# A weight's low part on GpSimd instead of VectorE, in attention with two networks behind it

## The chip, the cores and the metric

The kernel runs on one core of a Trainium2 chip. The metric is the time of one execution on the device, in microseconds (us). Its engines are TensorE (PE in the rows, PEld for its weight loads), VectorE (DVE), ScalarE (ACT), GpSimd (POOL) and SyncE (SP, which issues transfers). Each engine works through its own queue in order; a semaphore holds an instruction until what it needs is there, and everything behind it on the same engine waits too.

## What is computed

Attention over 2 batches, 8 heads, 768 positions and 64 columns with a window of 128 positions and 4 sink positions, then a network with a squared ReLU, then one with a rational function. Inputs are float32 or float64; the weights come as float64.

```python
def _attn_ref(q, k, v, n_sink, window):
    scores = scale * np.matmul(q, k.transpose(0, 1, 3, 2))
    keep = is_sink | in_window
    scores = np.where(keep, scores, -1000000000.0)
    scores = scores - np.max(scores, axis=-1, keepdims=True)
    a = np.exp(scores)
    a = a / (np.sum(a, axis=-1, keepdims=True) + 1e-09)
    return np.matmul(a, v).astype(np.float32)
...
def _moe_ref(x, w_in, w_out):            # x: 1536 x 512, w_in: 512 x 2048, w_out: 2048 x 512
    h = x @ w_in
    r = np.maximum(h, 0.0)
    g = r * r
    return (g @ w_out).astype(np.float32)
...
def _moe2_ref(x, w_in, w_out, a, b):
    h = x @ w_in
    h2 = h * h
    h3 = h2 * h
    P = a[0] + a[1] * h + a[2] * h2 + a[3] * h3
    Q = 1.0 + np.abs(b[0]) * np.abs(h) + np.abs(b[1]) * h2
    g = P / (Q + 1e-06)
    return (g @ w_out).astype(np.float32)
```

## The kernel before

**Stages.** The 1536 rows of tokens are four groups of 512, 256, 256 and 512. Attention is cut into 24 units of two heads by two blocks of 128 queries. The eight units of group 0 run at the start, up to about 56 us. From then on the first network works on group 0, later on groups 1, 2 and 3, and the units of the later groups are put between its steps, piece by piece. Behind it, from about 370 us, stands the second network.

**A unit of attention.** Scores (line 298) on TensorE; mask and row minimum on VectorE (line 307); exponential with row sums on ScalarE (line 309, four to a unit); reciprocal of the sums on VectorE (lines 312, 313); scaling by them (line 317), two pieces on GpSimd and two on VectorE; transposes on TensorE (line 330), whose results are copied out as `pT0` by ScalarE and as `pT1` by VectorE (line 332); product with the values (line 345), copied out as `xhi` and `xlo` (lines 350, 351) or `x` (line 353).

**Products in two parts.** A float32 product is three products of a fast type: each operand is split in a high part, rounded, and a low part, the remainder. A step of the first network takes 128 of the 2048 middle columns: `gemm1` multiplies `whi` by `xhi`, `whi` by `xlo` and `wlo` by `xhi` (lines 411 to 413), `act1` makes the square of the ReLU as `ghi` and `glo` (lines 420 to 423), and `gemm2a` multiplies these by the second matrix two steps later (lines 434, 435 and 440).

**A weight's conversion.** A weight tile of 128x512 comes as float64 by one transfer of 512 KB into `st` (three buffers). `to_f32` makes a float32 of it: ScalarE casts the top half-word into `top` (line 135, a single buffer), VectorE shifts and combines `st` and `top` into `wt` (line 136, two buffers). Then `w_split_` has ScalarE round it to `whi` (line 395) and VectorE take `wlo` = `wt` - `whi` (line 396). There are 64 such conversions, 32 for each network. Of the first network's, seven run during the units at the start (`CONV`), and 25 in the steps of group 0, from about 58 to 127 us; all stay in SBUF. The second network's 32 run later, from within the last group on.

**What sets the order.** A scheduler lays out the queues of VectorE, ScalarE, GpSimd and SyncE. TensorE's queue is written by hand up to group 2. `issue_after(op)` lets the scheduler place an instruction only behind the named one. The conversions of the first network are held behind the mask (`lastV`) and the exponentials (`lastA`) of a recent piece of attention in this way: `va_hist` keeps these two for each piece, and `w_split` takes those of three pieces ago.

Of the kernel before, what the change touches and what calls it, by code (L numbers as in the profile page):

```python
# [10 lines left out]
F32 = mybir.dt.float32  # L11
# [6 lines left out]
ALU = mybir.AluOpType  # L18
# [20 lines left out]
NORM_POOL = (0,)  # L39
# [24 lines left out]
def seg_dims(seg):  # L64

    _, blk0, nb = seg
    assert nb == 2
    return (2 * KB + P, nb * P, 3 * P, 4 * P) if blk0 > 0 else (KB + P, nb * P, 2 * P, 2 * P)


def key_cols(seg, i, j):

    _, blk0, _ = seg
    if blk0 == 0 and i == 0:
        return 0, P
    return (i if blk0 > 0 else 0) * KB + j * D, WQ
# [52 lines left out]
def to_f32(nc, st, t, top):  # L129

    mid = st.bitcast(I32)[:, 1 : 1 + 2 * WH].rearrange("p (n w) -> p n w", w=2)[:, :, 0]
    head = st.bitcast(BF16)[:, 4 : 4 + 4 * WH].rearrange("p (n w) -> p n w", w=4)[:, :, 0]
    nc.scalar.copy(top.bitcast(F16).rearrange("p (n w) -> p n w", w=2)[:, :, 1], head)  # L135
    nc.vector.scalar_tensor_tensor(t.bitcast(I32), in0=mid, scalar=13, in1=top,  # L136
                                   op0=ALU.logical_shift_right, op1=ALU.bitwise_or)
# [20 lines left out]
class Fast:  # L158
# [116 lines left out]
    def att_unit(self, u, raws, alt):  # L275


        nc = self.nc
        tags = self.alt_tags(alt)
        V, A, G = nc.vector, nc.scalar, nc.gpsimd  # L280
        g, c, seg, xo = u
        b, blk0, nb = seg
        wk, wq, wa, wb = seg_dims(seg)
        n = nb * P
        raw, vv = raws
        kr, qr = raw[:, :wk], raw[:, wk:]
        rows = [slice(D * k, D * k + D) for k in range(2)]
        ws = [key_cols(seg, i, 0)[1] for i in range(nb)]
        os = [sum(ws[:i]) for i in range(nb)]
        pt = self.att.tile([P, 2, 2 * WQ], F32, tag="p", name="p", bufs=2)  # L290
        sums = self.const.tile([P, 4], F32, tag="sums", name="sums", bufs=6)
        sc = [self.att_bank() for _ in range(2)]
        for i in range(nb):
            for k, r in enumerate(rows):
                for j in range(2):
                    q0 = i * P + j * D
                    off, w = key_cols(seg, i, j)
                    nc.tensor.matmul(sc[k][j * D : j * D + D, os[i] : os[i] + w], qr[r, q0 : q0 + D],  # L298
                                     kr[r, off : off + w], start=True, stop=True, skip_group_check=True)
        for i in range(nb):  # L300
            m = self.m2 if blk0 > 0 else (self.m0, self.m1)[i]
            for k in range(2):
                mn = self.mn[:, self.mn_i : self.mn_i + 1]
                self.mn_i += 1
                cs = slice(os[i], os[i] + ws[i])
                p = pt[:, k, cs]
                self.lastV = V.tensor_tensor_reduce(p, sc[k][:, cs], m, scale=-0.125, scalar=3.0e38,  # L307
                                                    op0=ALU.add, op1=ALU.min, accum_out=mn)
                self.lastA = A.activation(p, p, AF.Exp, scale=-1.0, bias=mn,  # L309
                                          accum_out=sums[:, k * nb + i : k * nb + i + 1])  # L310
        yield
        V.tensor_scalar_add(sums[:, : 2 * nb], sums[:, : 2 * nb], 1e-9)
        V.reciprocal(sums[:, : 2 * nb], sums[:, : 2 * nb])  # L313
        for i in range(nb):
            for k in range(2):
                p = pt[:, k, os[i] : os[i] + ws[i]]
                (G if i in NORM_POOL else V).tensor_scalar(p, p, sums[:, k * nb + i : k * nb + i + 1], 0.0,  # L317
                                                           op0=ALU.mult, op1=ALU.add)
        if g:
            for _ in range(ST_T):  # L320
                yield
            vv = self.att_load_v(u, 0)
        yield
        heads = [i for i in range(nb) if ws[i] == WQ]
        pieces = [os[i] + x for i in range(nb) for x in ((0, P - NSK) if i in heads else (0,))]
        pT = []
        for k in range(2):
            tb = self.att_bank()
            for j, o in enumerate(pieces):
                nc.tensor.transpose(tb[:, j * P : (j + 1) * P], pt[:, k, o : o + P], self.ident)  # L330
            t = self.att_tile(f"pT{k}", len(pieces) * P, alt=tags[k])
            (A.copy if k == 0 else V.tensor_copy)(t, tb[:, : len(pieces) * P])
            pT.append(t)
        yield
        va, vb = (t.rearrange("p (j d) -> p j d", d=D) for t in vv)
        ob = self.att_bank()
        if blk0 > 0:
            jobs = [(va, 0, 0, 0, D), (vb, 0, P, 0, D), (vb, 1, D, D, D), (va, 1, P + D, D, P)]
        else:
            jobs = [(va, 0, 0, 0, P + D)]  # L340
        y, pp = 2 * len(heads) - 2, (len(pieces) - 2) * P
        jobs += [(vb, y, pp + P, P, D), (vb, y + 1, pp + D, P + D, D), (va, len(heads), pp + P + D, P + D, D)]
        for n_, (vt, vi, pp, q0, w) in enumerate(jobs):
            for k, r in enumerate(rows):
                nc.tensor.matmul(ob[r, q0 : q0 + w], vt[:, 2 * vi + k], pT[k][:, pp : pp + w], start=n_ == 0,  # L345
                                 stop=n_ == len(jobs) - 1, skip_group_check=True)
        xs = slice(xo, xo + n)
        if g == 0:
            xhi, xlo = self.x[g]
            A.copy(xhi[:, c, xs], ob[:, :n])  # L350
            V.tensor_tensor(xlo[:, c, xs], ob[:, :n], xhi[:, c, xs].bitcast(F32), op=ALU.subtract)
        else:
            A.copy(self.x32[g][:, c, xs], ob[:, :n])
        yield
# [32 lines left out]
    def w_split_(self, which, f, half):  # L387
        nc = self.nc
        st = self.wst.pop((which, f, half))
        t = self.stage.tile([P, WH], F32, tag="wt", name="wt", bufs=2)  # L390
        to_f32(nc, st, t, self.tops[self.conv_i % NTOP])
        self.conv_i += 1
        whi = self.wp.tile([P, WH], F32R, tag=f"whi{f}_{half}", name="whi")
        wlo = self.wp.tile([P, WH], F32R, tag=f"wlo{f}_{half}", name="wlo")
        nc.scalar.copy(whi, t)  # L395
        nc.vector.tensor_tensor(wlo, t, whi.bitcast(F32), op=ALU.subtract)  # L396
        self.w[(which, f, half)] = (whi, wlo)


# [76 lines left out]
    def run(self, ctx):  # L476
        tc, nc = self.tc, self.nc
        V, A = nc.vector, nc.scalar
# [8 lines left out]
        self.psum = mk(root, "psum", 1, None, space=bass.MemoryType.PSUM)  # L487
        self.att_banks, self.h_banks = [0, 1, 2, 3, 6, 7], [4, 5]
        self.att_i = self.h_i = 0
        self.lastV = self.lastA = None  # L490
        self.va_hist = []
        self.a2i = 0
        self.x, self.x32, self.w, self.wst = {}, {}, {}, {}
# [35 lines left out]
        def tick():  # L529
            with ExitStack() as c:  # L530
                if urgent:
                    c.enter_context(tc.high_priority(offset=HP))
                tick_()
            self.va_hist.append((self.lastV, self.lastA))

        def tick_():
            nonlocal done, tick_no, ui
# [61 lines left out]
        with tc.manual_schedule(engines={mybir.EngineType.PE}):  # L599
            for k in range(n0 + 1):  # L600
                if k == 0:
                    wload(0, 3)
                if k < n0:
                    u, raws = loaded.pop(0)
                    g0[k] = self.att_unit(u, raws, k % NALT)
                    for _ in range(2):
                        next(g0[k])
                if k:
                    with tc.high_priority(offset=HP0):
                        next(g0[k - 1])  # L610
                while k >= 2 and pc < (k - 1) // per:
                    for f in range(HEAD):
                        self.gemm1_part(0, f, pc, self.x[0], GN[0], hb[f])
                    pc += 1
                if k:
                    with tc.high_priority(offset=HP0):
                        next(g0[k - 1])
                with ExitStack() as cc:
                    cc.enter_context(tc.issue_after(self.lastV.ins))
                    cc.enter_context(tc.issue_after(self.lastA.ins))  # L620
                    for _ in range(CONV[k]):
                        wconv(*cq[0][0])
                while nload < n0 and len(loaded) < DEPTH - 1 or not loaded:
                    prefetch()
            done = n0
# [133 lines left out]
        for i in range(len(steps) + 1):  # L759
            if i < len(steps):  # L760
                which, t, f = steps[i]
# [253 lines left out]
```

## Time and profile before

| | us |
|---|---|
| time, median of three runs | 639.09 (638.14 to 640.57) |
| time of the profiled execution | 640.31 |
| its span in the profile | 638.5 |
| TensorE busy in it | 614.0 |
| VectorE busy | 417.3 |
| ScalarE busy | 416.9 |
| GpSimd busy | 109.1 |

The profile is of one execution. Its span runs from the first to the last instruction; the time of that execution is 1.8 us longer. TensorE is busy for 96% of the span, VectorE and ScalarE for 65% each, GpSimd for 17%. These shares are means over stages that differ, so the rows below take the stages apart. In the rows, "idle before" is the time an engine stood still ahead of an instruction, and behind the arrow stands the instruction that released it.

### The profile page before, as it was taken

The page shows a single profiled execution, that of the slowest core. Times are in us where ns is not written, and L with a number is a line of the kernel's source. Part 1 is how long each engine was busy: PE and PEld are TensorE (multiplying, and loading weights), DVE is VectorE, ACT ScalarE, POOL GpSimd, SP SyncE. Part 2 cuts the span into 40 slices and gives each one's busy share as a digit, 9 for nine tenths or more (in the row PEclk, how much of TensorE's full clock was granted, in tenths as well). Part 3 has the DMA queues.
Part 4 walks back from the last instruction along what each step waited for, and adds up shares of the span by engine and source line. Part 5 has one row for each costly group of instructions (what it writes and reads, how often), then busy time and mean ns, then how long its engine had stood idle before and what let it go on. Part 6 is the DMA issues. An engine that isn't in the chain of part 4 may idle for free.

```text
span 638.5 us, 10295 instructions
## 1 busy us (share of the span) xinstructions
PE 614.0 (96%) x3841; PEld 513.2 (80%) x3841; DVE 417.3 (65%) x854; ACT 416.9 (65%) x896; POOL 109.1 (17%) x123
## 2 busy tenths in 40 slices
PE   4698999999999999999999999999999999999996
PEld 3466777877999899998888888888888888888885
DVE  6766887733242353346666559998788777877773
ACT  4567888845454555456777768777676666766663
POOL 2110000000010011021000003434223332222221
PEclk9888999999999999999999999999999999999998
DMA  8734677621221232003555500000010000100001
GB/s 291 272 114 148 220 235 249 225 88 35 57 76 52 82 106 80 1 1 133 184 191 193 191 1 1 1 0 1 0 67 2 0 1 0 55 12 2 1 1 69
DMA packets 19351, 54.86 MB, mean 86 GB/s; under 512 B 2528, under 2 KB 3808, under 8 KB 19296
## 3 DMA queue, kind: packets, MB, share of 16 engines
q1 hardware_dynamic: 19008, 54.01, 25.4%
q8 instruction: 32, 0.52, 0.4%
q14 instruction: 23, 0.19, 0.1%
q10 hardware_dynamic: 288, 0.13, 0.1%
HBM read 50.99 MB, written 3.15 MB: 85 GB/s over the span
## 4 chain that ended last, share of the span: by engine, by line
PE 92%; ACT 3%; DVE 3%; DMA 1%; issue 0%; POOL 0%; POOLq 0%
PE b L411 14%; PE b L413 13%; PE b L412 13%; PE b L434 7%; PE b L440 7%; PE b L435 7%; PE b L473 7%; PE b L472 7%; PE b L471 7%; PE b L345 4%; PE b L298 3%; PE b L330 2%; ACT p L309 2%; DVE p L307 1%; DMA nsw<-nsw 1%
## 5 line engine op out<-in xcount | busy, mean ns | idle before, releaser
L411 PE MATMUL b<-xhi,whi 128*128 128x512 f32 (+1 forms) x320 | 113.7, 356 | 0.5 <-ACT xhi L350 0.5
L412 PE MATMUL b<-xlo,whi 128*128 128x512 f32 (+1 forms) x320 | 111.8, 349 | 0.0
L413 PE MATMUL b<-xhi,wlo 128*128 128x512 f32 (+1 forms) x320 | 111.7, 349 | 0.0
L423 DVE TENSOR_TENSOR glo<-b,ghi 128x512 fp32r<-128x512 f32 (+1 forms) x64 | 35.5, 555 | 76.4 <-ACT b L422 76.2
L434 PE MATMUL b<-ghi,whi 128*128 128x512 f32 (+1 forms) x256 | 83.7, 343 | 0.8 <-ACT ghi L421 0.8
L435 PE MATMUL b<-ghi,wlo 128*128 128x512 f32 (+1 forms) x256 | 81.9, 336 | 0.0
L462 POOL TENSOR_TENSOR glo<-t,ghi 128x512 fp32r<-128x512 f32 x34 | 45.0, 1323 | 213.6 <-ACT ghi L461 187.2
L472 PE MATMUL b<-wlo,ghi 128*128 128x512 f32 x192 | 74.7, 389 | 0.0
L471 PE MATMUL b<-whi,ghi 128*128 128x512 f32 x192 | 74.4, 389 | 0.0
L473 PE MATMUL b<-whi,glo 128*128 128x512 f32 x192 | 71.9, 389 | 0.0
L411 PEld LDWEIGHTS b<-xhi,whi 128*128 128x128 f32 x320 | 60.8, 190 | 10.7 <-issue 2.2
L413 PEld LDWEIGHTS b<-xhi,wlo 128*128 128x128 f32 x320 | 60.9, 190 | 7.7
L412 PEld LDWEIGHTS b<-xlo,whi 128*128 128x128 f32 x320 | 60.9, 190 | 7.3
L317 POOL TENSOR_SCALAR p<-p,sums 128x224 f32<-128x224 f32 (+1 forms) x48 | 25.4, 541 | 232.8 <-DVE sums L313 127.4
L309 ACT ACTIVATE p<-p,mn 128x224 f32<-128x224 f32 (+1 forms) x96 | 43.9, 459 | 32.1 <-DVE mn L307 32.0
L396 DVE TENSOR_TENSOR wlo<-wt,whi 128x512 fp32r<-128x512 f32 x64 | 44.7, 699 | 25.5 <-ACT whi L395 25.2
L395 ACT CAST whi<-wt 128x512 fp32r<-128x512 f32 x64 | 39.5, 618 | 33.3 <-PE b L412 21.1
L420 ACT ACTIVATE b<-b 128x512 f32<-128x512 f32 (+1 forms) x64 | 31.0, 486 | 43.6 <-PE b L413 43.6
L440 PE MATMUL b<-glo,whi 128*128 128x512 f32 (+1 forms) x256 | 55.9, 340 | 0.0
L434 PEld LDWEIGHTS b<-ghi,whi 128*128 128x128 f32 x256 | 48.4, 189 | 8.4 <-issue 2.0
L435 PEld LDWEIGHTS b<-ghi,wlo 128*128 128x128 f32 x256 | 48.5, 189 | 4.9
L135 ACT CAST top<-st 128x512 f16<-128x512 bf16 x64 | 49.7, 776 | 1.0 <-DVE wt L136 1.0
(128 smaller groups left out, 1242.0 us busy)
## 6 DMA issues: line engine op xcount, KB each, us to landing
st<-w SPq DMA_DIRECT2D x64, 512.0 KB, 3.5
vv<-att SPq DMA_DIRECT2D x12, 448.0 KB, 3.3
raw<-att SPq DMA_DIRECT2D x12, 352.0 KB, 3.2
out<-o SPq DMA_DIRECT2D x8, 256.0 KB, 2.1
raw<-att SPq DMA_DIRECT2D x6, 272.0 KB, 3.8
vv<-att SPq DMA_DIRECT2D x6, 256.0 KB, 3.7
raw_e<-att SPq DMA_DIRECT2D x4, 352.0 KB, 5.5
vb<-att SPq DMA_DIRECT2D x4, 256.0 KB, 4.5
```

What stands on the lines that cost most here:

```text
L135: nc.scalar.copy(top.bitcast(F16).rearrange("p (n w) -> p n w", w=2)[:, :, 1], head)
L309: self.lastA = A.activation(p, p, AF.Exp, scale=-1.0, bias=mn, accum_out=sums[:, k * nb + i : k * nb + i + 1])
L411: nc.tensor.matmul(h[:, :n], whi[:, cs], xhi[:, c, :n], start=(c == 0), stop=False)
L412: nc.tensor.matmul(h[:, :n], whi[:, cs], xlo[:, c, :n], start=False, stop=False)
L413: nc.tensor.matmul(h[:, :n], wlo[:, cs], xhi[:, c, :n], start=False, stop=(c == NC - 1))
L434: nc.tensor.matmul(acc[m], whi[:, ms], ghi, start=(f == 0 and not pk), stop=pk, **kw)
L435: nc.tensor.matmul(acc[m], wlo[:, ms], ghi, start=False, stop=pk, **kw)
L440: nc.tensor.matmul(acc[m], whi[:, ms], glo, start=False, stop=pk or f == NF - 1, **kw)
L462: self.lastL = nc.gpsimd.tensor_tensor(glo, t3, ghi.bitcast(F32), op=ALU.subtract)
L471: nc.tensor.matmul(acc[t], ghi[:, ts_], whi, start=(f == 0), stop=False)
L472: nc.tensor.matmul(acc[t], ghi[:, ts_], wlo, start=False, stop=False)
L473: self.lastM = nc.tensor.matmul(acc[t], glo[:, ts_], whi, start=False, stop=(f == NF - 1))
```

## The change

The subtraction of line 396 goes to GpSimd where the weight is one of the first network's (`which` is 0); the second network's stay on VectorE. The last scaling that a unit of attention puts on GpSimd (line 317) is remembered as `lastP`, and a conversion is held behind it as it is behind `lastV` and `lastA`. Line numbers from 319 on are two higher in the changed kernel, those from 490 on up to three (the subtraction is line 398 there).

```diff
--- before.py
+++ after.py
@@ -314,8 +314,10 @@
         for i in range(nb):
             for k in range(2):
                 p = pt[:, k, os[i] : os[i] + ws[i]]
-                (G if i in NORM_POOL else V).tensor_scalar(p, p, sums[:, k * nb + i : k * nb + i + 1], 0.0,
-                                                           op0=ALU.mult, op1=ALU.add)
+                op = (G if i in NORM_POOL else V).tensor_scalar(p, p, sums[:, k * nb + i : k * nb + i + 1], 0.0,
+                                                                op0=ALU.mult, op1=ALU.add)
+                if i in NORM_POOL:
+                    self.lastP = op
         if g:
             for _ in range(ST_T):
                 yield
@@ -393,7 +395,7 @@
         whi = self.wp.tile([P, WH], F32R, tag=f"whi{f}_{half}", name="whi")
         wlo = self.wp.tile([P, WH], F32R, tag=f"wlo{f}_{half}", name="wlo")
         nc.scalar.copy(whi, t)
-        nc.vector.tensor_tensor(wlo, t, whi.bitcast(F32), op=ALU.subtract)
+        (nc.vector if which else nc.gpsimd).tensor_tensor(wlo, t, whi.bitcast(F32), op=ALU.subtract)
         self.w[(which, f, half)] = (whi, wlo)
 
 
@@ -487,7 +489,7 @@
         self.psum = mk(root, "psum", 1, None, space=bass.MemoryType.PSUM)
         self.att_banks, self.h_banks = [0, 1, 2, 3, 6, 7], [4, 5]
         self.att_i = self.h_i = 0
-        self.lastV = self.lastA = None
+        self.lastV = self.lastA = self.lastP = None
         self.va_hist = []
         self.a2i = 0
         self.x, self.x32, self.w, self.wst = {}, {}, {}, {}
@@ -531,7 +533,7 @@
                 if urgent:
                     c.enter_context(tc.high_priority(offset=HP))
                 tick_()
-            self.va_hist.append((self.lastV, self.lastA))
+            self.va_hist.append((self.lastV, self.lastA, self.lastP))
 
         def tick_():
             nonlocal done, tick_no, ui
@@ -618,6 +620,7 @@
                 with ExitStack() as cc:
                     cc.enter_context(tc.issue_after(self.lastV.ins))
                     cc.enter_context(tc.issue_after(self.lastA.ins))
+                    cc.enter_context(tc.issue_after(self.lastP.ins))
                     for _ in range(CONV[k]):
                         wconv(*cq[0][0])
                 while nload < n0 and len(loaded) < DEPTH - 1 or not loaded:
```

The scheduler gives all queues but the pinned one of TensorE anew. TensorE's order stays. In the rows of the order below, numbers behind a name tell buffers of the same name apart.

**GpSimd, from the units at the start to the end of group 0's steps.** `p` are a unit's exponentials, `sums` their reciprocals, `wlo` the low parts. The queue of the kernel before:

```order
L317 TENSOR_SCALAR p_577<-p_577,sums_578 128x224 x2
L317 TENSOR_SCALAR p_834<-p_834,sums_835 128x224 x2
L317 TENSOR_SCALAR p_988<-p_988,sums_989 128x224 x2
L317 TENSOR_SCALAR p_1167<-p_1167,sums_1168 128x224 x2
L317 TENSOR_SCALAR p_1353<-p_1353,sums_1354 128x224 x2
```

The same stretch of the changed one:

```order
L398 TENSOR_TENSOR wlo_828<-wt_824,whi_827 128x512
L317 TENSOR_SCALAR p_834<-p_834,sums_835 128x224 x2
L398 TENSOR_TENSOR wlo_879<-wt_875,whi_878 128x512
L398 TENSOR_TENSOR wlo_906<-wt_902,whi_905 128x512
L398 TENSOR_TENSOR wlo_934<-wt_930,whi_933 128x512
L398 TENSOR_TENSOR wlo_955<-wt_951,whi_954 128x512
L398 TENSOR_TENSOR wlo_983<-wt_979,whi_982 128x512
L398 TENSOR_TENSOR wlo_1028<-wt_1024,whi_1027 128x512
L317 TENSOR_SCALAR p_988<-p_988,sums_989 128x224 x2
L398 TENSOR_TENSOR wlo_1056<-wt_1052,whi_1055 128x512
L398 TENSOR_TENSOR wlo_1097<-wt_1093,whi_1096 128x512
```

Between two pairs of scalings there are now five to seven subtractions.

**ScalarE, where the first network takes over from the units at the start.** `b4`, `b5`, `b6` are the results of `gemm1`, `ghi_701` is the high part of the first step's squared ReLU. Before:

```order
L420 ACTIVATE b5_154<-b5_154 128x512
L421 ACTIVATE ghi_701<-b4_153 128x512
L422 ACTIVATE b4_153<-b4_153 128x512
L395 CAST whi_716<-wt_713 128x512
L135 CAST top0_104<-st_681 128x512
```

And now:

```order
L422 ACTIVATE b5_154<-b5_154 128x512
L397 CAST whi_716<-wt_713 128x512
L135 CAST top0_104<-st_681 128x512
L423 ACTIVATE ghi_701<-b4_153 128x512
L424 ACTIVATE b4_153<-b4_153 128x512
```

A cast and a `top` have moved ahead of `ghi_701`.

**ScalarE, ahead of the copy `pT0_1072`** of the second unit between group 0's steps, for which TensorE waits in line 345. Before:

```order
L309 ACTIVATE p_988,sums_989<-p_988,mn_150 128x224 x4
L395 CAST whi_1027<-wt_1024 128x512
L135 CAST top0_104<-st_958 128x512
L420 ACTIVATE b4_1033<-b4_1033 128x512
L395 CAST whi_1055<-wt_1052 128x512
L135 CAST top0_104<-st_986 128x512
L332 COPY pT0_1072<-b6_1067 128x512
```

And now:

```order
L397 CAST whi_1027<-wt_1024 128x512
L135 CAST top0_104<-st_958 128x512
L309 ACTIVATE p_988,sums_989<-p_988,mn_150 128x224 x2
L397 CAST whi_1055<-wt_1052 128x512
L135 CAST top0_104<-st_986 128x512
L422 ACTIVATE b4_1033<-b4_1033 128x512
L397 CAST whi_1096<-wt_1093 128x512
L334 COPY pT0_1072<-b6_1067 128x512
```

The cast `whi_1096` has come ahead of the copy.

## Rows read from the trace of the kernel before

**Rows 1.** Busy time by stretches (start:end, length, each engine's busy us with count, clock, DMA)
```profile
0.00:58.00 58.00, 41.13 (x393) 29.52 (x394) 38.81 (x153) 32.09 (x96) 10.98 (x27) 0.88 0.63 214
58.00:127.00 69.00, 68.24 (x404) 53.80 (x404) 52.18 (x115) 59.90 (x126) 5.84 (x8) 1.00 0.66 223
```
**Rows 2.** Waits (waiting instruction <- what released it: us, times, longest)
```profile
ACT whi L395 <- DVE wt L136: 12.1, 16, 1.2
```
**Rows 3.** One loop of conversions, ScalarE, then VectorE (start, us, instruction [idle before])
```profile
95.90 0.62 ACT L395 CAST whi<-wt 128x512 fp32r<-128x512 f32 x1 [0.54 <-DVE wt L136]
96.43 0.79 ACT L135 CAST top<-st 128x512 f16<-128x512 bf16 x1
97.97 0.62 ACT L395 CAST whi<-wt 128x512 fp32r<-128x512 f32 x1 [0.76 <-DVE wt L136]
...
96.56 0.69 DVE L396 TENSOR_TENSOR wlo<-wt,whi 128x512 fp32r<-128x512 f32 x1 [0.69 <-ACT whi L395]
97.25 0.69 DVE L136 SCALAR_TENSOR_TENSOR wt<-st,top 128x512 int32<-128x512 int32 x1
```
**Rows 4.** Lines 136 and 462 (count: ns least/median/most, first and last start)
```profile
L136 DVE SCALAR_TENSOR_TENSOR wt<-st,top x64: 673/693/1669, 14.7 to 397.1; 128x512 int32<-128x512 int32 x64
...
L462 POOL TENSOR_TENSOR glo<-t,ghi x34: 1291/1299/1622, 380.1 to 624.7; 128x512 fp32r<-128x512 f32 x34
```
**Rows 5.** GpSimd and VectorE side by side in the last group
```profile
385.61 1.30 POOL L462 TENSOR_TENSOR glo<-t,ghi 128x512 fp32r<-128x512 f32 x1 [4.20 <-ACT ghi L461]
...
386.25 1.20 DVE L136 SCALAR_TENSOR_TENSOR wt<-st,top 128x512 int32<-128x512 int32 x1
```
**Rows 6.** ScalarE and TensorE at the start of group 0's second products
```profile
58.97 0.61 ACT L421 ACTIVATE ghi<-b 128x512 fp32r<-128x512 f32 x1
...
59.96 0.63 ACT L395 CAST whi<-wt 128x512 fp32r<-128x512 f32 x1
60.47 0.80 ACT L135 CAST top<-st 128x512 f16<-128x512 bf16 x1
61.10 0.65 ACT L420 ACTIVATE b<-b 128x512 f32<-128x512 f32 x1
...
59.63 0.50 PE L434 MATMUL b<-ghi,whi 128*128 128x512 f32 x1 [0.76 <-ACT ghi L421]
```
**Rows 7.** ScalarE, a unit's four exponentials: the first, and the cast behind them
```profile
86.61 0.47 ACT L309 ACTIVATE p<-p,mn 128x224 f32<-128x224 f32 x1
...
88.47 0.61 ACT L395 CAST whi<-wt 128x512 fp32r<-128x512 f32 x1
```
**Rows 8.** ScalarE's copy `pT0_1072` and the TensorE work that takes it
```profile
92.39 0.56 ACT L332 COPY pT<-b 128x512 f32<-128x512 f32 x1
...
93.00 0.68 PE L345 MATMUL b<-pT,vv 128*64 128x64 f32 x14
```
**Rows 9.** The same for `pT0_1429`
```profile
125.70 0.59 ACT L332 COPY pT<-b 128x512 f32<-128x512 f32 x1
...
126.87 0.34 PE L345 MATMUL b<-pT,vv 128*64 128x64 f32 x4
```
**Rows 10.** GpSimd, one pair of scalings
```profile
106.59 1.46 POOL L317 TENSOR_SCALAR p<-p,sums 128x224 f32<-128x224 f32 x2 [15.96 <-ACT whi L395]
```
**Rows 11.** VectorE and TensorE at two places of the start
```profile
29.02 0.69 DVE L396 TENSOR_TENSOR wlo<-wt,whi 128x512 fp32r<-128x512 f32 x1 [0.69 <-ACT whi L395]
29.63 0.42 DVE L351 TENSOR_TENSOR xlo<-b,xhi 128x256 fp32r<-128x256 f32 x1
...
41.87 0.68 DVE L396 TENSOR_TENSOR wlo<-wt,whi 128x512 fp32r<-128x512 f32 x1
42.48 0.68 DVE L332 COPY pT<-b 128x512 f32<-128x512 f32 x1
...
43.21 0.27 PE L345 MATMUL b<-pT,va 128*64 128x64 f32 x1 [0.71 <-DVE pT L332]
```
**Rows 12.** Busy time by stretches again, around the clock's fall (columns as in rows 1)
```profile
31.00:32.00 1.00, 0.00 (x0) 0.00 (x0) 0.69 (x3) 1.00 (x5) 0.00 (x0) 0.57 1.08 299
32.00:37.00 5.00, 4.85 (x51) 3.83 (x51) 2.51 (x12) 1.54 (x7) 0.78 (x2) 0.50 0.49 161
```

## The prediction, made before the changed kernel was run

> **What bounds the kernel now.** I read the busy table by stretches first [rows 1]. From 58 to 127 us, where 25 of the 32 moved subtractions stand, TensorE works 68.24 of 69.00 us: nearly without a gap, but ScalarE is close behind it with 59.90 us, and VectorE has 52.18. GpSimd is almost free (5.84). So TensorE bounds this stretch, and ScalarE is the engine that would take over. In the first 58 us TensorE works 41.13 us and has real holes. The other seven subtractions are there. After 127 us none of the moved ones is left; TensorE is full there, so that a delay made before 127 us is carried to the end.
>
> Next, who waits for whom [rows 2]. ScalarE waited 16 times, 12.1 us in all, for the combine of line 136 before its own cast of line 395. The loop of a weight is thus limited by its chain, not by the work of an engine: the rows of one loop [rows 3] show the cast at 95.90, the subtraction on VectorE at 96.56, the next weight's combine at 97.25, and the next cast at 97.97. That is 2.07 us from cast to cast. The subtraction costs nothing extra there, because ScalarE makes the next `top` at the same time (96.43, 0.79 us): it ends at 97.22, the subtraction at 97.25.
>
> **The change part by part.** *What VectorE loses:* 32 subtractions of 0.69 us [rows 3]. In the loop this relieves nothing, since `top` ends at the same time as the subtraction did.
>
> *What GpSimd gets:* 32 subtractions of two SBUF inputs, 128x512. The trace has this form on GpSimd in line 462: 1291 ns at the least, 1299 in the median and 1622 at the most [rows 4]. I take 1.30; the least is so near that the price has no low end worth keeping.
>
> *What the move does to the loop.* Here is the main term. The combine of the next weight stands on VectorE and also reads two SBUF tiles (`st` and `top`). At 385.61 GpSimd starts a line 462 and takes 1.30, until 386.91; VectorE's combine starts at 386.25 and takes 1.20, until 387.45 [rows 5]. Its median over 64 is 0.69 [rows 4]. So it ended 0.54 after GpSimd's instruction and hardly got on before that. In the changed loop, the subtraction becomes ready with the end of the cast, and the combine with the end of `top`, 0.70 us later: always inside GpSimd's 1.30. A loop is then cast 0.62, some 0.04 to GpSimd's start, 1.30, 0.54, and 0.03 to the next cast, 2.53 us instead of 2.07: **+0.46** for each loop that is limited by the chain. Other VectorE work (line 423, which reads PSUM) is only queued behind the combine.
>
> [...]
>
> ScalarE's order in the change lets me lay the loops end to end. The prices are distances of starts: two activations of 512 columns 0.99, cast 0.51, `top` 0.63 [rows 6], four exponentials of a unit 1.86 [rows 7].
>
> *Handover, 59.6 us.* TensorE waits 0.76 us for the first `ghi` of group 0, which ScalarE starts at 58.97 [rows 6]. In the change a cast and a `top` (`whi_716`, st_681) stand ahead of it: 0.51 + 0.63, **+1.14**.
>
> *First stretch, from that `ghi` (`ghi_701`) to `pT0_1072`.* Five activations come to 2.48 before the cast `whi_725`. From there to `whi_1096` are twelve loops. Nine have so little between that the chain sets them: 9 x 2.53 = 22.77. Three have more on ScalarE than the chain lasts: 4.49 (0.51 + 1.86 + 0.63 + 1.49), 2.63 and 3.06 (0.51 + 0.63 + 0.99 + 0.93). Sum 32.95. With the last cast's 0.51, 35.94 us. Before it is 92.39 - 58.97 = 33.42 [rows 6, 8]. The difference, 2.52, has two sources: one more conversion (`whi_1096`) stands ahead of `pT0_1072` now, and loops are longer. With the handover `pT0_1072` starts 3.66 us later, at 96.05. TensorE can't cover it: the copy ends at 92.95, and line 345 takes `pT0_1072` at 93.00 [rows 8]; the slack is 0.05. So by there **+3.66**.
>
> *Second stretch, to `pT0_1429`.* Eleven loops from `whi_1096` to `whi_1590`: five set by the chain (12.65), three of 2.63, one each of 3.00 and 3.03 with more on ScalarE, one of 5.39 with a unit's exponentials and three activations. Then 3.16 to the copy, since a second `top` waits there for the held combine. That is 35.12, less the 0.51 already counted: 34.61 against 125.70 - 92.39 = 33.31 [rows 8, 9], +1.30. That copy ends at 126.29 and line 345 takes it at 126.87 [rows 9], so there is 0.5 more of slack: **+0.8**, sum +4.5.
>
> *GpSimd's queue.* The order ties a subtraction behind the unit's scaling. Three pairs of line 317 (p_988, p_1167, p_1353) have subtractions close behind them. A pair lasts 1.46 us [rows 10]; a subtraction that finds one running starts later, and with it the end of the hold, by 0 to about 1.0 (the loop's spare time aside). I take 0.5 each, **+1.5**: half way, since no row says where in a loop of the change a pair falls.
>
> *Start, 0 to 58 us.* Seven subtractions. For: VectorE does one ahead of `pT` at 41.87, and TensorE waits 0.71 for that `pT` until 43.21 [rows 11]; without it about -0.5. Another, at 29.02, stands ahead of `xlo` (29.63) [rows 11]; without it `xlo` and the unit's masking behind it start up to 0.6 earlier, of which I take 0.4, -0.4. Against: holds at the earlier combines, where the subtraction on GpSimd meets one about 0.5 each, one or two of which reach TensorE. I take **0**, between -0.9 and +1.
>
> Sum: 1.14 + 2.52 + 0.8 + 1.5 + 0 = +6.0. The profiled execution took 640.31 us (span 638.5), 1.22 above the median of 639.09; put on the median, 639.09 + 6.0 = **645.1**. Ends: pairs that cost nothing and a start that gains 0.9 leave 3.6; pairs at 1.0 each and a start that loses 1 make 8.5. The forecast's own range is thus 642.7 to 647.6.
>
> **The rivals.**
> (a) *The hold bites little.* [...] For it: only 12.1 us of waiting is on the combine [rows 2]; against it: [rows 5], and a loop has only 2.07 us. What remains is the handover's 1.14 less 0.4 at the start: 639.8.
> [...]
> [...]
> [...] That the change doesn't do what it says is out: the order of GpSimd shows the subtractions of the first network there.
>
> **How the numbers follow.** Forecast 0.55, (a) 0.22, (b) 0.09, (c) 0.10, (d) 0.04. Half a per cent, about what a measurement can tell from no change, is 3.2 us: slower from 642.3. Slower is the forecast, (b) and (c), 0.74; (a) and (d) lie within half a per cent, 0.26, of which 0.03 goes to faster, for a relief larger than that of (d). The range goes from 639.5, which takes in most of (a), to 648.5, past the centres of (b) and (c).
>
> **What would show it.** In the changed profile: line 136 at about 1.2 us each between 58 and 127 us instead of 0.69, line 398 on GpSimd near 1.3, casts about 2.5 us apart in the plain loops, ScalarE's wait for line 136 grown from 12 to over 20 us, and TensorE waiting 0.76 + 1.1 for the first `ghi` and some 2.5 for `pT0` near 95 us. If line 136 keeps 0.7 us, the main term is wrong. If it is 1.2 us and TensorE in 58 to 127 us has no new gap, then ScalarE had slack that I didn't see. [...]

## The result, and the profile of the changed kernel

The changed kernel takes 648.33 us in the median of four runs (647.17 to 649.35), the kernel before 638.66 beside it (638.14 to 640.57): a ratio of 1.0144, 95% interval 1.0122 to 1.0166. The forecast was 645.1 with a range of 639.5 to 648.5. The profiled execution of the change took 648.29 us (span 646.5), that of before 640.31 (span 638.5), so the two traces differ by 8.0 us.

Busy time by stretches of the change, to be held against [rows 1] (start:end, length, busy us of PE, PEld, DVE, ACT and POOL with counts, granted clock, DMA):

```profile
0.00:58.00 58.00, 40.04 (x396) 28.44 (x396) 36.06 (x146) 33.01 (x98) 19.92 (x34) 0.91 0.63 211
58.00:127.00 69.00, 63.71 (x358) 50.40 (x359) 42.16 (x80) 54.12 (x112) 34.63 (x30) 0.93 0.65 212
```

From 58 to 127 us VectorE is busy for 10 us less, and TensorE gets through less all the same: 63.71 instead of 68.24 us busy, at a clock of 0.93 instead of 1.00. ScalarE, which was at 59.90, is at 54.12: not busier, but kept waiting. The waits of the whole execution tell for what. ScalarE's wait for the combine, 12.1 us in [rows 2], is now 19.9; below it stands TensorE's wait for the copies `pT0`, in the change and then before:

```profile
ACT whi L397 <- DVE wt L136: 19.9, 22, 1.4
...
PE b L347 <- ACT pT L334: 10.5, 6, 3.6
```

```profile
PE b L345 <- ACT pT L332: 6.2, 5, 2.9
```

A plain loop (one that the chain sets), as in [rows 3], on ScalarE, GpSimd and VectorE. An activation on ScalarE at 86.84 is left out; it fits into ScalarE's idle time:

```profile
85.67 0.62 ACT L397 CAST whi<-wt 128x512 fp32r<-128x512 f32 x1 [1.26 <-DVE wt L136]
86.20 0.78 ACT L135 CAST top<-st 128x512 f16<-128x512 bf16 x1
...
88.24 0.62 ACT L397 CAST whi<-wt 128x512 fp32r<-128x512 f32 x1 [0.77 <-DVE wt L136]
...
86.37 1.29 POOL L398 TENSOR_TENSOR wlo<-wt,whi 128x512 fp32r<-128x512 f32 x1 [1.28 <-ACT whi L397]
...
87.06 1.14 DVE L136 SCALAR_TENSOR_TENSOR wt<-st,top 128x512 int32<-128x512 int32 x1 [1.43 <-ACT top L135]
```

The subtraction runs until 87.66; the combine, ready at 87.06, ends at 88.20, 0.54 later; the next cast starts 0.04 behind it. From cast to cast it is 2.57 us, before 2.07. Over all 64 combines the mean went from 738 to 913 ns.

TensorE newly waits in two places. The first is the handover of [rows 6], ScalarE and then TensorE:

```profile
58.27 0.62 ACT L397 CAST whi<-wt 128x512 fp32r<-128x512 f32 x1 [0.30 <-DVE wt L136]
58.80 0.77 ACT L135 CAST top<-st 128x512 f16<-128x512 bf16 x1
59.44 0.58 ACT L423 ACTIVATE ghi<-b 128x512 fp32r<-128x512 f32 x1
...
60.06 0.79 PE L436 MATMUL b<-ghi,whi 128*128 128x512 f32 x1 [2.34 <-ACT ghi L423]
```

The second is the copy of [rows 8] (`pT0_1072`; the text on the order gives it to the second unit between the steps, but it belongs to the first, p_834):

```profile
97.61 0.58 ACT L334 COPY pT<-b 128x512 f32<-128x512 f32 x1
...
98.25 1.98 PE L347 MATMUL b<-pT,vv 128*64 128x64 f32 x28 [3.23 <-ACT pT L334]
```

Behind both waits the granted clock fell from 1.00, to 0.51 (60 to 62 us) and to 0.50 (98 to 104 us; stretches as above, the first a mean over both clocks):

```profile
60.00:65.00 5.00, 4.94 (x15) 3.96 (x16) 3.81 (x5) 4.67 (x11) 1.52 (x2) 0.66 0.49 167
...
98.00:101.00 3.00, 2.75 (x30) 2.54 (x31) 1.38 (x2) 3.00 (x7) 1.64 (x2) 0.50 0.68 199
101.00:103.00 2.00, 2.00 (x6) 1.52 (x6) 1.15 (x1) 0.96 (x4) 0.72 (x2) 0.50 0.91 332
```

### The profile page after: what moved, and what is told of

Same layout as the page of the kernel before. It is cut to its first block, busy times and chain, and to the rows that moved or that the text cites. A ratio compares the mean times of both kernels' runs of the same rounds, so it can differ in the third digit from the quotient of the medians.

```text
span 646.5 us, 10296 instructions
## 1 busy us (share of the span) xinstructions
PE 616.5 (95%) x3841; PEld 515.4 (80%) x3841; DVE 408.6 (63%) x822; ACT 417.3 (65%) x896; POOL 149.6 (23%) x155
## 4 chain that ended last, share of the span: by engine, by line
PE 83%; DVE 1%; ACT 1%; issue 0%; POOL 0%; POOLq 0%; ACTq 0%
PE b L413 13%; PE b L414 12%; PE b L415 12%; PE b L474 7%; PE b L475 7%; PE b L473 7%; PE b L436 6%; PE b L442 6%; PE b L437 6%; PE b L347 3%; PE b L298 2%; PE b L332 2%; DVE wt L136 0%; ACT p L309 0%; ACT y L660 0%
## 5 line engine op out<-in xcount | busy, mean ns | idle before, releaser
L136 DVE SCALAR_TENSOR_TENSOR wt<-st,top 128x512 int32<-128x512 int32 x64 | 58.4, 913 | 26.7 <-ACT top L135 17.1
```

## The experiments

One number comes near to ordering them: when the 25 conversions of the steps are through. The last cast of line 395 (`whi_1590`) stands on ScalarE ahead of the copy `pT0_1429` [rows 9], and TensorE needs that copy for its next product. From this product to the span's end it is 511.6 us before (638.5 - 126.87) and 511.6 in the change (646.5 - 134.93), so that what the change costs is lost ahead of it. These are the last cast before, and in the change the last cast, the copy and its product:

```profile
123.97 0.62 ACT L395 CAST whi<-wt 128x512 fp32r<-128x512 f32 x1 [1.20 <-DVE wt L136]
```

```profile
130.29 0.62 ACT L397 CAST whi<-wt 128x512 fp32r<-128x512 f32 x1 [1.20 <-DVE wt L136]
...
133.50 0.57 ACT L334 COPY pT<-b 128x512 f32<-128x512 f32 x1
...
134.93 1.14 PE L347 MATMUL b<-pT,vv 128*64 128x64 f32 x28
```

Starts of these instructions in the profiled executions, us, with the median of the runs and its ratio to the runs of the kernel before that were made beside them:

| kernel | first cast of the steps | last cast | between | product | median | ratio (95%) |
|---|---|---|---|---|---|---|
| before | 59.96 | 123.97 | 64.0 | 126.87 | 638.66 to 639.65 | |
| changed | 58.27 | 130.29 | 72.0 | 134.93 | 648.33 | 1.0144 (1.0122 to 1.0166) |
| e1_start_only | 59.99 | 125.83 | 65.8 | 129.00 | 642.35 | 1.0054 (1.0037 to 1.0071) |
| e2_steps_only | 57.92 | 126.97 | 69.1 | 130.83 | 645.32 | 1.0107 (1.0086 to 1.0127) |
| e6_extra | 62.26 | 139.72 | 77.5 | 142.06 | 659.45 | 1.0322 (1.0304 to 1.0340) |
| e8_halves | 56.02 | 124.05 | 68.0 | 127.58 | 641.70 | 1.0040 (1.0023 to 1.0057) |
| e9_start_ghi | 61.84 | 123.48 | 61.6 | 125.84 | 639.78 | 1.0010 (0.9989 to 1.0032) |
| e10_all_ghi | 61.95 | 130.14 | 68.2 | 132.48 | 645.73 | 1.0091 (1.0063 to 1.0119) |
| e11_late | 60.46 | 125.53 | 65.1 | 127.89 | 642.34 | 1.0050 (1.0029 to 1.0070) |
| e12_halves_ghi | 62.23 | 127.69 | 65.5 | 130.03 | 644.89 | 1.0089 (1.0066 to 1.0112) |

Two things limit this table. The profiled execution of the kernel before lost 1.5 us to the clock at 50 us (0.66 from 50 to 55 us, last section), so that a product that starts a little ahead of its 126.87, as in e9, is no gain by itself. And in e6, e10, e11 and e12 TensorE, once it has begun that product, waits again for `pT1` from VectorE (1.00, 0.51, 1.46 and 0.19 us); from the product to the end it is 515.1 us in e6, 514.3 in e11 and 514.5 in e12, and 511.4 to 512.5 in the others.

**Which of the 32.** e1 and e2 each move a part:

```diff
-(nc.vector if which else nc.gpsimd).tensor_tensor(wlo, ...)
+(nc.gpsimd if which == 0 and self.conv_i <= 7 else nc.vector).tensor_tensor(wlo, ...)   # e1
+(nc.gpsimd if which == 0 and self.conv_i > 7 else nc.vector).tensor_tensor(wlo, ...)    # e2
```

> The changed kernel with only the seven subtractions of the start on GpSimd; the 25 in the steps of group 0 are on VectorE again. Theory (the hold of the combine in the steps makes the loss): in the steps the casts are 2.07 us apart again in the plain loops and line 136 takes 0.69; the handover still has a cast and a top ahead of the first ghi, about 1.1 us; time 639 to 641.5. Rival (the order at the handover and the clock's fall behind it make most of the loss): this kernel keeps that order, so 644 or more.

> The changed kernel with only the 25 subtractions of the steps on GpSimd, the seven of the start on VectorE. Its queue on ScalarE has the first ghi ahead of the cast, as before the change, and pT0 of the first unit ahead of whi_1096. Theory: plain loops of 2.57 us, line 136 at 1.15; pT0 some 3 to 3.5 us later than before (92.39), TensorE waits for it in one piece, and the clock falls behind it as in the changed kernel; 644 to 646, or about 642.5 if the clock holds. Rival (handover): 639 to 640.

e1: 642.35, a little above what its theory gave (639 to 641.5) and below the rival (644). Its plain loops are back at 2.05 and its combines at 0.69, as expected; TensorE waits 2.35 us for the first `ghi`, as in the change. e2: 645.32, as its theory had it. Its first `ghi` comes as before (wait 0.76), its loops are 2.57, and the wait and the clock behind it are there:

```profile
93.53 1.98 PE L347 MATMUL b<-pT,vv 128*64 128x64 f32 x28 [2.56 <-ACT pT L334]
...
93.00:99.00 6.00, 5.46 (x36) 4.61 (x37) 3.31 (x4) 4.23 (x8) 3.07 (x3) 0.50 0.60 193
```

Each against its own runs of the kernel before, e2 costs 6.4 us and e1 3.4, together about the change's 9.7: the larger part is the steps'.

**Do the two engines hold each other up?** e6 leaves the kernel before as it is and adds an instruction on GpSimd that no one waits for:

```diff
 nc.vector.tensor_tensor(wlo, t, whi.bitcast(F32), op=ALU.subtract)
+if which == 0:
+    spare = self.att.tile([P, WH], BF16, tag="spare", name="spare", bufs=1)
+    nc.gpsimd.tensor_tensor(spare, t, whi.bitcast(F32), op=ALU.subtract)
```

> The kernel before, with one more instruction on GpSimd for each conversion of the first network: the same subtraction into a spare tile (bfloat16) that nobody reads. Queues of the other engines stand as before. [...] Rival (only dependences count): nobody waits for the extra subtraction, 639 and loops of 2.07.

659.45, where the rival had 639: the two engines hold each other up although neither waits for the other's result. Two casts on ScalarE, VectorE's subtraction and combine, and GpSimd's extra instruction between them:

```profile
69.11 0.62 ACT L395 CAST whi<-wt 128x512 fp32r<-128x512 f32 x1 [0.84 <-DVE wt L136]
...
72.17 0.62 ACT L395 CAST whi<-wt 128x512 fp32r<-128x512 f32 x1 [0.82 <-DVE wt L136]
...
69.77 0.69 DVE L396 TENSOR_TENSOR wlo<-wt,whi 128x512 fp32r<-128x512 f32 x1 [0.69 <-ACT whi L395]
70.51 1.63 DVE L136 SCALAR_TENSOR_TENSOR wt<-st,top 128x512 int32<-128x512 int32 x1
...
69.88 1.72 POOL L399 TENSOR_TENSOR spare<-wt,whi 128x512 bf16<-128x512 f32 x1 [1.34 <-ACT whi L395]
```

VectorE came first by 0.11 us, so that GpSimd's 1.30 became 1.72; then it was the combine's turn to be held, until 0.54 after GpSimd's end. It is 3.06 us from cast to cast; the prediction's loop with VectorE's subtraction of [rows 3] in it (0.62 + 0.04 + 1.3 + 0.54 + 0.69) gives an estimate of about 3.2. The extra instruction does read `wt`, so a later combine must wait until that buffer is free, but no such wait shows in this loop: the combine had begun and was held while it ran. Not all of the 20 us are in the loops; TensorE also waits 2.71 and 2.14 us behind masks of line 307 that VectorE gets to later.

**Which forms are held?** e5 and e5b give the combine one input, so that the weights, and the results, are other numbers:

```diff
-nc.vector.scalar_tensor_tensor(t.bitcast(I32), in0=mid, scalar=13, in1=top, ...)
+nc.vector.tensor_scalar(t.bitcast(I32), top, 13, None, op0=ALU.logical_shift_right)         # e5
+nc.vector.tensor_scalar(t, top.bitcast(F32), sc, 0.0, op0=ALU.mult, op1=ALU.add)            # e5b
```

> The changed kernel, but the combine of the first network's weights reads only top and no st (their middle word is left out, so the weights are other numbers); it still waits for the same cast. Theory (GpSimd's instruction blocks a combine of two SBUF inputs): the combine takes 0.7 or less beside GpSimd's subtraction, plain loops of 2.1 us or less instead of 2.57; the order has two casts ahead of the first ghi, about 2.3 us, so 640 to 644. Rival (what counts is how long GpSimd's subtraction takes, or another wait in the loop): loops stay at 2.57 and the time at 648.

> The changed kernel, but the combine of the first network's weights is the form of a scaling (line 317: one SBUF input, a column of factors), so that the weights are other numbers; it still waits for the same cast. [...] Rival (VectorE is blocked whenever GpSimd works in SBUF): loops of 2.3 or more and 644 or more.

e5: 644.74, just above the theory's 644, and its numbers for the combine and the loop were wrong: 0.87, not 0.7 or less, and 2.30, not 2.1 or less. Two of its combines on VectorE, the first beside GpSimd's subtraction, the second alone, and that subtraction:

```profile
78.91 0.87 DVE L137 TENSOR_SCALAR wt<-top 128x512 int32<-128x512 int32 x1 [1.43 <-ACT top L135]
...
89.65 0.43 DVE L137 TENSOR_SCALAR wt<-top 128x512 int32<-128x512 int32 x1
...
78.21 1.29 POOL L401 TENSOR_TENSOR wlo<-wt,whi 128x512 fp32r<-128x512 f32 x1 [1.01 <-ACT whi L400]
```

Alone it takes 0.43; held, it ends 0.28 after GpSimd. With two inputs it was 0.69 and 0.54. In both, what is left to do after GpSimd's end is the instruction's own time less 0.15 us. e5b (644.53, loops 2.30) was to be a form that isn't held; it ran in 0.48 at the shortest and in 0.87 beside GpSimd, so it was held too, and the rival's numbers (2.3 and 644) came true. Which form of a combine would pass beside GpSimd stays open. What did pass is an instruction that has one of its two inputs in PSUM: in e6, the subtraction for `glo` took the 0.68 that it takes alone, all inside GpSimd's:

```profile
94.42 1.29 POOL L399 TENSOR_TENSOR spare<-wt,whi 128x512 bf16<-128x512 f32 x1 [1.34 <-ACT whi L395]
...
94.80 0.68 DVE L426 TENSOR_TENSOR glo<-b,ghi 128x512 fp32r<-128x512 f32 x1
```

**The meeting, or GpSimd's slowness?** e11 keeps the steps' subtractions on GpSimd, each behind the next weight's combine (GpSimd first copies one column of the next `wt`):

```diff
+if self.late is not None:
+    a, b, d = self.late
...
+    nc.gpsimd.tensor_copy(d[:, :1], t[:, :1])
+    nc.gpsimd.tensor_tensor(d, a, b.bitcast(F32), op=ALU.subtract)
+if which == 0 and 7 < self.conv_i < 32:
+    self.late = (t, whi, wlo)
...
```

> The 25 subtractions of the steps stay on GpSimd (the start's seven on VectorE, as in e2), but each is put behind the next weight's combine: GpSimd first copies one column of the next wt into the low part's tile, which it then overwrites. Theory (the loss of e2 is the meeting of subtraction and combine, not GpSimd's 1.3 us as such): the combine takes 0.69 again, plain loops 2.07 to 2.2, no wait for pT0 near 93 us, clock 1.00 there; 638 to 641 against 645.3 for e2. Rival (a subtraction on GpSimd costs wherever it stands, since it is slow or holds wt longer): loops of 2.5 and 644 or more.

642.34: between the theory (638 to 641) and the rival (644). The combine is at 0.69 again, and TensorE doesn't wait for `pT0_1072`. But loops are 2.2 to 2.6, since GpSimd now holds a `wt` buffer longer than VectorE did (its subtraction takes 1.30, VectorE's took 0.69), and the combine waits for that; later TensorE waits for a copy on VectorE (a combine, then TensorE's product):

```profile
77.88 0.69 DVE L136 SCALAR_TENSOR_TENSOR wt<-st,top 128x512 int32<-128x512 int32 x1 [1.19 <-POOL wlo L403]
...
129.68 1.13 PE L348 MATMUL b<-pT,vv 128*64 128x64 f32 x26 [1.46 <-DVE pT L335]
```

So about half of e2's 6.4 us went when subtraction and combine no longer met (e11 costs 3.2, interval 1.9 to 4.5). The rest goes with the buffer that a slower engine keeps for longer where there are two; the 25 added copies and the order of the queues were not told apart from it.

**A shorter hold.** e8 cuts each subtraction in two:

```diff
+e = WH // 2
+nc.gpsimd.tensor_tensor(wlo[:, :e], t[:, :e], whi[:, :e].bitcast(F32), op=ALU.subtract)
+nc.vector.tensor_tensor(wlo[:, e:], t[:, e:], whi[:, e:].bitcast(F32), op=ALU.subtract)
```

> The changed kernel with each of the 32 subtractions cut in two: columns 0 to 255 on GpSimd, 256 to 511 on VectorE. Theory (the hold lasts as long as GpSimd's instruction): GpSimd's half takes about 0.65 and ends with the top cast; VectorE's half is held beside it and ends some 0.2 later, then the combine runs in 0.69: plain loops of about 2.2 us; the handover keeps its 1.1 to 1.6; 641 to 644. Rival (two engines on each weight cost more in waits than the shorter hold saves): 646 or more.

641.70, as expected, with plain loops of 2.26, though the order was another: VectorE's half came first, GpSimd's half (0.73 at its shortest) was held, to 0.98, and held the combine a little, 0.83 instead of 0.69:

```profile
77.87 0.43 DVE L403 TENSOR_TENSOR wlo<-wt,whi 128x256 fp32r<-128x256 f32 x1 [0.69 <-ACT whi L397]
78.61 0.83 DVE L136 SCALAR_TENSOR_TENSOR wt<-st,top 128x512 int32<-128x512 int32 x1 [0.32 <-ACT top L135]
...
77.91 0.98 POOL L402 TENSOR_TENSOR wlo<-wt,whi 128x256 fp32r<-128x256 f32 x1 [1.62 <-ACT whi L397]
```

**The handover.** e9, e10 and e12 hold the first conversion of the steps behind a square of `act1`, on top of e1, of the change and of e8. In their traces nine activations of the first three steps, the first `ghi` among them, then stand ahead of its cast; in the change, e1 and e8 two do:

```diff
+self.lastS = nc.scalar.activation(r, r, AF.Square)
...
+if which == 0 and self.conv_i == 7:
+    c.enter_context(self.tc.issue_after(self.lastS.ins))
```

> e1 (only the start's seven subtractions on GpSimd) with the first conversion of the steps held behind the first ghi. Theory (most of e1's 3.4 us is the handover, where TensorE waits 2.35 instead of 0.76): wait of 0.7 to 0.8 there, plain loops of 2.07, 639.5 to 641. Rival (the start itself lost it, through combines held there): 642 or more.

> The changed kernel with the first conversion of the steps held behind the first ghi, so that ScalarE makes ghi first; its order then also has two fewer conversions ahead of the first unit's pT0 (whi_1055 and whi_1096 behind it). All 32 subtractions stay on GpSimd. Theory (each conversion ahead of pT0 costs a loop of 2.57): handover as before the change (0.8 us of wait), loops still 2.57, pT0 near 93 to 94 instead of 97.6, TensorE waits 1 to 2 us there; 639.5 to 643, the higher if the clock falls behind that wait. Rival (the hold costs wherever the conversions stand): 646 to 648.

> e8 (halves of each subtraction on GpSimd and VectorE) with the first conversion of the steps held behind the first ghi. Theory (the costs add: handover 2.6 us, which e1 against e9 and the change against e10 both gave; hold by the length of GpSimd's instruction): 641.7 less 2.6, so 638.5 to 640.5, no different from the kernel before; plain loops stay at 2.26 and TensorE waits 0.75 for the first ghi. Rival (VectorE's relief, 16 columns-halves a time, is worth something once the handover is mended): 637 or less.

e9: 639.78, as expected. TensorE's wait is 0.73 again, and the start's seven subtractions on GpSimd cost nothing that can be measured (0.6 us, interval -0.7 to +2.0):

```profile
58.41 0.50 PE L438 MATMUL b<-ghi,whi 128*128 128x512 f32 x1 [0.73 <-ACT ghi L425]
```

e10: 645.73, above the theory's 643 and just under its rival. `pT0_1072` came at 93.52, as worked out, but two conversions had only been put behind it, and the last copy was late again (131.85). e12: 644.89, where 638.5 to 640.5 was expected; it is slower than e8, which it was to mend. The idea behind that expectation, that the handover's 2.6 us (medians of e1 against e9, of the change against e10) can be taken off any of these kernels, is wrong. Holding the conversion back starts the chain of 25 later and, with those activations already done, also makes it shorter. By the table the start moves by 1.9 us in e9, 3.7 in e10 and 6.2 in e12, whose chain had begun ahead of the others' in e8 (56.02); the chain gets shorter by 4.2, 3.8 and 2.5. So the last cast comes 2.4 us earlier in e9, 0.2 earlier in e10 and 3.6 later in e12. (e10's product still comes 2.5 earlier: only one `top`, not two, stands between its last cast and the copy.) In e12 TensorE then waits further down the chain instead of at its beginning:

```profile
93.84 1.14 PE L347 MATMUL b<-pT,vv 128*64 128x64 f32 x28 [1.63 <-ACT pT L334]
...
130.03 0.33 PE L347 MATMUL b<-pT,vv 128*64 128x64 f32 x2 [2.25 <-ACT pT L334]
```

**The clock.** e7b and e7c put products that count for nothing where TensorE waits, here ahead of the product with `pT0_1072`; e7b also puts nine ahead of the first product with `ghi`:

```diff
...
+if self.nob == 9:
+    for q in range(13):
+        nc.tensor.matmul(ob, ..., start=True, stop=True)       # e7b: the bank of the product itself
+        nc.tensor.matmul(hx, ..., start=True, stop=True)       # e7c: a bank of gemm1 that is free
```

> The changed kernel with TensorE given work that counts for nothing where it waits: nine products of 512 columns (about 2 us) ahead of the first product with ghi, thirteen (about 3 us) ahead of the product with the first unit's pT0, all into banks that are overwritten. Theory (some 3.1 us behind 97 us and, in the profiled run, 1.7 behind 60 us were lost to the clock): granted clock 1.00 from 58 to 127 us, TensorE's waits shrink to a few tenths, and the time falls to 643 to 646. Rival (the clock falls for another reason, or the loss lies elsewhere): 648, or more by what the products overshoot.

> The changed kernel with thirteen products that count for nothing (about 3 us) ahead of the product with the first unit's pT0, into a bank that is free then (in e7b they had to wait for the copy themselves). Theory (3.1 us behind that wait are lost to the clock): TensorE's wait there falls under 1 us, the granted clock stays at 1.00 behind it, 644.5 to 646.5. Rival (the clock falls all the same, or the fall costs nothing because ScalarE is as late): 648 to 649.

e7b: 649.43, where 643 to 646 was its theory's. Its filling of the handover worked (wait 0.34, clock 1.00 from 58 to 66 us); the one at 95 us had to wait for the copy itself and tells nothing. e7c: 649.83, where its theory gave 644.5 to 646.5. Here TensorE had work (line 343) until 0.33 before the product, and the clock stayed at 1.00 behind it. It won nothing; TensorE waited elsewhere instead:

```profile
95.08 3.11 PE L343 MATMUL b<-xhi,whi 128*128 128x512 f32 x13
98.52 1.14 PE L352 MATMUL b<-pT,vv 128*64 128x64 f32 x28 [0.33 <-ACT pT L334]
...
106.72 0.97 PE L298 MATMUL b<-raw 64*64 64x224 f32 x12 [0.88 <-ACT x L360]
114.12 1.25 PE L332 MATMUL b<-ident,p 128*128 128x128 f32 x8 [1.67 <-DVE mn L307]
```

The rival (648 to 649) was right in kind: with the clock at 1.00 there the conversions were no earlier (its first cast at 58.47, its last at 131.64: 73.2 us between, 72.0 in the change). ScalarE's order differs behind 98 us in e7c, so the test isn't a pure one. The change's own trace bounds the matter: from the product with `pT0_1072` to that with `pT0_1429` TensorE needs 36.68 us without a wait, and 33.87 before, so the clock took 2.8; but the last copy ends at 134.07 and is taken at 134.93, so 0.9 at most could have been won.

**The tie.** The tie to `lastP` was not run by itself, so no run shows what it does alone. e2 has it, and up to the steps its trace shows the instructions of ScalarE, VectorE and GpSimd in the order of the kernel before.

## Why the prediction was right, and where it was off

The direction, the place and the hold of the combine were right; the size was short by 3.2 us. 648.33 lies outside the forecast's own 642.7 to 647.6 and inside the range only because that had been drawn past the centres of its rivals (b) and (c), so that it holds the result is partly luck. Of its signs, ScalarE's wait for the combine came to 19.9 where over 20 was named, and TensorE waited 3.23 for `pT0` near 95 us where some 2.5 was.

*The loop* was right: 2.57 measured against 2.53, with the held combines at 1.13 to 1.16 and GpSimd at 1.29. That the two engines hold each other up, argued from two rows, is shown by e6. What in the hardware makes the hold was not shown. The upper end of the range was set by two rivals: (b), a combine that runs whole, 0.69 us, behind GpSimd's subtraction, no run shows, since in the loop above it ended 0.54 behind it; (c) is taken up below.

*The handover* was right and a little larger: TensorE waited 2.34 instead of 0.76, 1.58 more against 1.14. The cast ahead of `ghi` had itself been held up by its combine, 0.30. On ScalarE it shows as 0.5 only (59.44 - 58.97), because TensorE began the steps 1.5 us earlier than in the trace of before, whose clock was low there (0.66 from 50 to 55 us, last section), and was still 1.2 us ahead where the wait began.

*The first stretch*, ScalarE from `ghi_701` to `pT0_1072`, went from 33.42 to 38.17 us: +4.75, where the sum had +2.52. This is the mis-sized term, 2.23 too small. 0.92 is in one loop, from the cast at 64.45 to that at 67.90 (2.53 in the sum): ScalarE waited there for products of a TensorE whose granted clock was 0.66 (60 to 65 us) after the handover's wait. 0.67 is in the loop from 93.89 to 97.09, where a pair of scalings stood ahead of the subtraction; that one the prediction had put under GpSimd's queue. The other ten loops were 0.02 to 0.20 longer each than worked out. The pair, GpSimd's subtraction behind it, and the combine:

```profile
94.32 0.96 POOL L317 TENSOR_SCALAR p<-p,sums 128x224 f32<-128x224 f32 x2 [1.02 <-DVE sums L313]
95.25 1.26 POOL L398 TENSOR_TENSOR wlo<-wt,whi 128x512 fp32r<-128x512 f32 x1
...
95.28 1.78 DVE L136 SCALAR_TENSOR_TENSOR wt<-st,top 128x512 int32<-128x512 int32 x1 [0.31 <-POOL p L317]
```

*The second stretch* went from 33.31 to 35.89, +2.58 against +1.30 and what was left of the pairs' 1.5. The 0.5 of slack that the sum took off at its end was not there to be used: TensorE, at a clock of 0.50 for 6 us, itself arrived 0.86 after the copy (0.58 before).

*The start* was taken as 0; e9 shows 0.1%, inside its interval. In the traces TensorE's 0.71 us wait for VectorE's `pT` [rows 11] is gone and its waits for ScalarE's have grown from 5.9 to 7.0. At 49.3 us the two stand level (49.34 and 49.39), but with the clock low at different places on the way (0.50 from 32 to 37 us before [rows 12], from 33 to 36 in the change), so the gains and the holds were not told apart.

*Rival (c)*, a fall of the clock behind TensorE's wait, came true, twice (0.51 and 0.50), and behind 97 us it took 2.8 us, and was still for the most part not an extra cost: TensorE, at 0.50 for 6 us, arrived little later than ScalarE's copy. What counts is the 0.92 that it gave back to ScalarE and the 0.86 at most at the end.

Added up on ScalarE: +0.5, then +4.75 and +2.58, in all 7.8; the product moved by 8.06, the span by 8.0, against a sum of 6.0. The rest of the miss, 1.2 us, is the step from the profiled execution to the median: that of before stood 1.22 above the median of 639.09, that of the change on its own (648.29 and 648.33), so the difference of the medians is larger than that of the traces. The 1.5 us that the trace of before lost to the clock at 50 us are about that much; that they are the cause is not shown.

## What to carry to other kernels

Before work goes from VectorE to GpSimd, look at what VectorE does while GpSimd works: here both took their inputs from SBUF and the same loop waited for VectorE, and GpSimd's 1.29 us entered the loop (2.07 to 2.57), however idle it had been (5.84 of 69 us), and even where nobody waited for its result (3.06 in e6). Find the point at which a chain of small jobs must be through, and how much slack it has there (0.5 us here): what lengthens each link is paid once that slack is used up. Mending the wait at the chain's head paid where the last cast came no later for it (e9, e10), and only moved the wait down the chain where it did (e12). A relief is worth something only on the engine for which the loop waits; here the subtractions of VectorE had been hidden behind a cast on ScalarE.

## What the runs showed of the hardware

In e6 the hold went both ways, by who started first: GpSimd's subtraction took 1.29 when it came first and 1.72 when VectorE's was 0.11 us ahead. A one-input instruction of VectorE was held as well, in two forms (0.43 to 0.87 in e5, 0.48 to 0.87 in e5b); one with an input in PSUM was not (0.68 beside GpSimd's 1.29, e6).

The granted clock of the start was not the same in each execution: 0.66, 1.00 and 1.00 from 50 to 55 us. The kernel before and e2 have the same instructions up to 58 us, and TensorE waits the same 1.06 and 0.30 us just before this stretch (before, then e2, then the change, where the waits are 1.07 and 0.30):

```profile
50.00:55.00 5.00, 4.70 (x17) 3.18 (x19) 3.60 (x7) 3.08 (x5) 0.24 (x1) 0.66 0.54 170
```

```profile
50.00:55.00 5.00, 4.54 (x43) 3.45 (x42) 3.69 (x6) 3.50 (x8) 0.00 (x0) 1.00 0.62 209
```

```profile
50.00:55.00 5.00, 4.29 (x42) 3.22 (x41) 2.70 (x5) 3.46 (x6) 2.75 (x3) 1.00 0.49 147
```

Before and the change come out of these waits at 49.34 and 49.39; the first product of the steps follows at 56.53 and 55.05, in e2 at 54.50:

```profile
56.53 0.96 PE L411 MATMUL b<-xhi,whi 128*128 128x512 f32 x3 [0.46 <-ACT xhi L350]
```

```profile
55.05 0.97 PE L413 MATMUL b<-xhi,whi 128*128 128x512 f32 x3 [0.46 <-ACT xhi L352]
```

Likewise a wait of 2.34 us at the handover was followed by a clock of 0.51 (60 to 62 us) in the change and one of 2.35 by 1.00 throughout in e1. So a microsecond or two of the start differed from one execution to the next here (1.5 between before and the change, 2.0 between before and e2), and a sum made against one profile carries that with it.
